# Reciprocal roots of layer norms moved to ScalarE as ln and exp, c loaded as rows, and a new order of the whole kernel

## The chip, the cores and the metric

The kernel runs on one core of a Trainium2 chip. The core has a matrix engine (TensorE, PE in the profile; its weight loads are PEld), a vector engine (VectorE, DVE), a scalar engine for table functions (ScalarE, ACT), a general engine (GpSimd, POOL), and a queue engine that issues transfers (SyncE, SP). Each engine works through its own list of instructions in order and waits on semaphores for the others. The metric is the device time of one execution in microseconds.

## The reference

x is 2048 rows of 448 values, c one row of 448. All weights and activations are bf16.

```
mod = silu(c) @ w_mod                       # six rows of 448: sa ca ga sb cb gb
h = layernorm(x) * (1 + ca) + sa
q, k, v = split(h @ wqkv)                   # 16 heads of 28
logits[i, w] = q[i] . k[i - 2 w] / sqrt(28) # w = 0..7, masked where i < 2 w
x = x + ga * ((softmax(logits) @ v) @ wo)
h = layernorm(x) * (1 + cb) + sb
y = layernorm(h)
x = x + gb * (gelu(y @ w1 + b1) @ w2 + b2)  # 1792 hidden values
layernorm(t) = (t - mean(t)) / sqrt(var(t) + 1e-5)
```

So there are three layer norms for each row: one ahead of the attention, two in a row ahead of the MLP.

## The kernel before

The 2048 rows are held as eight blocks of 128 partitions by two rows (s = 0 and 1, even and odd rows). The window of the attention steps by two rows, so even and odd rows never meet in it, and each is a sequence of 1024. Channels are split into seven pieces of 64 (`KB`), and two pieces lie on the 128 partitions at a time.

The plan is a list of operations, made by `build_plan`: each has a kind, the engines that may run it, what it reads and writes, and its PSUM buffers. There are four PSUM buffers of two banks. The sequence isn't worked out at run time: the text `ORDER` gives every operation's number and engine (P TensorE, D VectorE, A ScalarE, G GpSimd, S SyncE, X a transfer that has no instruction of its own), and `SLOTS` gives each buffer's place. An engine's own list is what `ORDER` says of it, and waits follow from reads, writes and buffers.

The stages, in the order in which they begin:

- **Start.** c is loaded into columns of 128 (`c_col`, two transfers on ACT's queue, L221 and L222, four bytes or less at a time). SyncE issues the loads of x, of w_mod and of the attention's weights. TensorE runs filler products (`fill`, L302). `f_silu` (L312) makes silu(c), `f_mcol` (L325) makes sa and ca as columns by 60 small products, and `f_mcev` brings them out of PSUM.
- **First norms.** Row blocks go in four groups of two (a0, a2, a4, a6). `ln_stats` (L349) takes mean and variance, on VectorE or, for some halves, on ScalarE (L357 to L359), adds eps (`tv`, L366), takes the power -0.5 on GpSimd (`rs`, L368) and makes -mean x rs (`nm`, L370). `normalize` (L373) writes z into `zb`. Blocks 0 to 3 are transposed on TensorE (L422), blocks 4 to 7 by a transposing transfer (L435). `modulate` (L391) applies 1 + ca and sa on the way to `hT`.
- **Weight copy.** The weights of Q and K are copied from `wst` into `wqk` with each 28 columns padded to 32 (`wpad`, L239 to L253), ten copies of 896 columns that go to VectorE, ScalarE or GpSimd.
- **Projections and attention.** `qk` (L451) makes Q and K in three chunks of columns (0 to 255, 256 to 511, 512 to 1023); in the first chunk Q's two PSUM buffers are filled piece by piece as `hT` arrives. `qkev` evicts them. `vproj` makes V in nine blocks of 114 columns (`v`, evicted by `vev`), `attention` makes logits (`lt`), their exp on ScalarE, the mask, the product with V (`po`), the division (`rec`, `onm`) and a transposition (`otr`, evicted by `oev`); `wo` is the output projection and adds to x.
- **MLP.** It runs in four chunks of two row blocks. `ln2` (L625) does both norms of a block with the functions above and transposes the result by transfer (L646, `yT`). `w1` (L666) fills a buffer, GELU on ScalarE evicts it (L673), 14 times for each chunk; `w2` (L690) follows, and `fin` (L699) adds.

ScalarE's functions come from table sets, and a load (ACT_TABLE_LOAD in the profile) stands where the next function isn't in the set that is loaded; exp and gelu are in different ones, while copies and scalings need none.

Of the kernel before, what the change touches and what calls it, by code (L numbers as in the profile page):

```python
# [8 lines left out]
FP32 = mybir.dt.float32  # L9
BF16 = mybir.dt.bfloat16  # L10
ACTF = mybir.ActivationFunctionType
# [3 lines left out]
KB = 7  # L15
# [8 lines left out]
KM = 4  # L24
# [4 lines left out]
 'fill1': 17,  # L29
 'fill2': 0,  # L30
 'fill3': 2,
# [9 lines left out]
60D 1A 49G 5S 0D 61D 68P 7S 3A 2X 6X 67G 9S 62A 8X 65G 11S 4X 10X 13S 66G 15S 17S 75D 19S 63G 76A 74D 12X 21S 64G 77D 23S 14X 69A 78D 25S 70D 79G 16X  # L41
27S 72P 71G 18X 80D 81D 82A 20X 85G 50D 52A 29S 53D 84G 51D 31S 83P 22X 73A 59G 57D 33S 86P 58A 55G 141P 24X 87D 88A 35S 56G 26X 90D 54G 142P 89A 143P
106D 28X 144P 92D 151P 30X 107A 120D 32X 34X 91D 145P 153P 105D 93G 104A 94G 152D 146P 147P 95D 119D 154A 148P 99G 208P 150D 96G 36X 149A 108D 100A
210P 97D 109G 209D 98P 110D 211A 122D 116G 226P 111A 37S 115D 112G 240P 121D 101P 227A 117S 38X 123G 241A 102D 197P 124G 113S 118X 103A 242D 237P 229P
114X 125D 228D 238A 39S 212P 130D 126A 40X 239D 198A 214P 131D 213A 199S 132S 243P 127A 215A 161P 128S 133X 230A 155P 41S 129X 162D 43S 42X 231D 45S
44X 157P 156A 47S 46X 140G 200S 48X 138D 139A 137D 201S 136G 135D 232P 134A 179S 159P 233D 158A 244D 234D 180X 165P 160A 245D 202G 203D 253P 166A 250P
163P 254A 251A 255D 181S 235P 246P 164A 252D 171P 182X 247D 236A 256P 172A 248P 257D 258D 206P 249D 183S 259P 173P 260A 184X 207D 342D 405G 341D 261P
174A 343G 169P 344G 262D 345D 360D 346G 175P 170A 185S 347D 412G 359D 186X 263P 348D 176A 266P 167P 349D 264A 361G 351D 362G 267A 177P 350D 168A 187S
363D 268D 365G 188X 364A 352D 265D 216P 353G 178A 366D 354D 269P 367D 217A 355G 279P 356D 276P 369D 280A 357S 218P 368D 277A 189S 358X 281D 220P 370G
219A 371G 278D 190X 270D 222P 372D 221A 271D 374G 373A 282P 223A 375S 272P 283D 224P 284D 273A 191S 376X 274P 225A 192X 285P 275D 385P 286A 381P 420D  # L50
287P 419D 193S 386A 204D 421G 194X 382A 383P 422G 391P 384A 288D 403P 392A 379P 423D 438D 404A 195S 401P 437D 380A 377P 196X 424D 402A 439G 425D 440G
395P 426D 378A 397P 441D 427D 396A 443G 442D 387P 398A 428D 389P 388A 429D 399P 390A 205D 430G 393P 431G 400A 305P 394A 292P 432D 444D 289P 433G 406P
# [104 lines left out]
def build_plan(cfg):  # L157
# [57 lines left out]
    def load_m(a, b, nm, bulk=False):  # L215

        load("SP", 3 * 256 * (b - a) * D, lambda g, e: e.dma_start(out=g.wmod[:, 0:3, a * D:b * D], in_=g.w_mod[0:384, a * D:b * D].rearrange("(kt p) n -> p kt n", p=128)), [(nm, 0, 3)], issue=0.65, bulk=bulk)
        load("SP", 256 * (b - a) * D, lambda g, e: e.dma_start(out=g.wmod[:, 3, a * D:b * D], in_=g.w_mod[320:448, a * D:b * D]), [(nm, 3, 4)], issue=0.42, at=lambda g: g.wmod[0:1, 3, a * D:a * D + 1])

    op("ms", {"DVE": 0.12}, lambda g: g.nc.vector.memset(g.c_col[0:64, 3:4], 0.0), wr=[("c_col", 2, 3)], bump=5000.0)  # L220
    load("ACT", 900, lambda g, e: e.dma_start(out=g.c_col[:, 0:3], in_=g.c[:, 0:384].rearrange("o (kt p) -> p (o kt)", p=128)), [("c_col", 0, 1)], issue=0.45)  # L221
    load("ACT", 900, lambda g, e: e.dma_start(out=g.c_col[64:128, 3:4], in_=g.c[:, 384:448].rearrange("o p -> p o")), [("c_col", 1, 2)], issue=0.45)  # L222
# [5 lines left out]
    load("SP", 229376, lambda g, e: e.dma_start(out=g.wst[:, 3], in_=g.A_wqkv[320:448, 0:2 * D]), [("wqk", 3, 4)], issue=0.45)  # L228
# [10 lines left out]
    for kb in range(KB):  # L239
        lo, up = ((3, k - 5) if k >= 5 else (k // 2, k % 2) for k in (kb, (kb + 1) % KB))  # L240
        if kb == 4:
            up = (2, 1)
        for halves in ([(0, 128, lo[0], 0)] if lo[0] == up[0] and (lo[1], up[1]) == (0, 1) else [(0, 64, *lo), (64, 64, *up)]):
            def f(g, kb=kb, x=halves, e=None):
                p0, n, i, h = x
                dst = g.wqk[p0:p0 + n, kb].rearrange("p m (r e) -> p (m r) e", e=32)[:, :, 0:DH]
                src = g.wst[64 * h:64 * h + n, i, :].rearrange("p (r d) -> p r d", d=DH)
                if e == "ACT":
                    g.nc.scalar.copy(out=dst, in_=src)
                else:  # L250
                    (g.nc.vector if e == "DVE" else g.nc.gpsimd).tensor_copy(out=dst, in_=src)  # L251
            i = halves[2]
# [652 lines left out]
```

## Time and profile before

| what | value |
|---|---|
| median of three runs | 180.21 us (177.99 to 181.09) |
| the profiled execution | 177.12 us, of which the span from first to last instruction is 175.4 us |
| busy share of the span | TensorE 93%, VectorE 64%, ScalarE 61%, GpSimd 39% |
| granted TensorE clock, mean | 0.99 |
| table loads on ScalarE | 6 of 1.28 us |
| first projection of Q and K | at 12.81 us |
| first `w1` product | at 72.13 us |
| first `w1` product of the second chunk | at 97.95 us |
| last `w2` product ends | at 172.05 us |

Busy shares are averages over stages with different limits. The groups of a page give busy time and the mean duration of one instruction; behind the second bar is the idle time of the engine just ahead of these instructions, with what ended it. An engine that idles costs nothing unless the last chain of work runs through it.

### The profile page before, as it was taken

How to read it: one execution, taken by the hardware profiler on the slowest of the kernel's cores; microseconds unless marked ns; L12 is line 12 of the kernel's file. 1: busy time of each engine (PE TensorE's matmuls, PEld its weight loads, DVE VectorE, ACT ScalarE, POOL GpSimd, SP SyncE). 2: the span in 40 equal slices, each digit the busy share in tenths (PEclk: the TensorE clock that was granted, in tenths of full speed). 3: DMA queues.
4: the chain of work that ended last, by engine and by line, in shares of the span. 5: the costliest groups of instructions: out<-in, count | busy, mean ns of one | idle time of the engine just before them, and what ended most of it. 6: DMA issues, size and time to landing. Idle time of an engine off the chain costs nothing.

```text
span 175.4 us, 7205 instructions
## 1 busy us (share of the span) xinstructions
PE 163.5 (93%) x3235; PEld 111.4 (64%) x3236; DVE 112.6 (64%) x234; ACT 106.9 (61%) x155; POOL 68.8 (39%) x99
## 2 busy tenths in 40 slices
PE   7889987999779988999999999999999999999992
PEld 2367754875335476699655877755589754886550
DVE  0699995594868988549798656996699812001203
ACT  2489987688334797788923686983268610686000
POOL 7594760030265454023676404623423754000400
PEclk9969999999999999999999999999999999999999
DMA  4999759628345408532024200003400044000202
GB/s 68 365 381 351 281 120 124 133 54 257 103 181 209 108 15 174 109 109 78 4 41 87 90 6 4 4 6 56 105 4 0 4 104 105 6 0 4 78 0 78
DMA packets 20939, 17.56 MB, mean 100 GB/s; under 512 B 12328, under 2 KB 19372, under 8 KB 20908
## 3 DMA queue, kind: packets, MB, share of 16 engines
q1 hardware_dynamic: 20428, 17.10, 35.3%
q8 instruction: 25, 0.41, 1.0%
q10 hardware_dynamic: 480, 0.00, 0.1%
q14 instruction: 6, 0.05, 0.1%
HBM read 12.51 MB, written 1.84 MB: 82 GB/s over the span
## 4 chain that ended last, share of the span: by engine, by line
PE 59%; DVE 15%; DMA 11%; ACT 4%; issue 4%; POOL 4%; SPq 0%; ACTq 0%; POOLq 0%; DVEq 0%
PE ps L666 25%; PE ps L690 19%; PE ps L465 7%; DMA yT<-zb 6%; DVE st L361 5%; PE ps L617 4%; DMA x_all<-in_A_x_dram 3%; DMA hT<-zb 3%; POOL rs L368 2%; PE ps L541 2%; PE ps L570 1%; DVE mv L362 1%; ACT et L549 1%; DVE zb L382 1%; DVE w L251 1%
## 5 line engine op out<-in xcount | busy, mean ns | idle before, releaser
L673 ACT ACTIVATE hmw<-ps,b1c 128x512 bf16<-128x512 f32 x56 | 38.1, 687 | 15.8 <-PE ps L666 12.6
L666 PE MATMUL ps<-yT,w 64*128 64x256 bf16 x784 | 44.4, 269 | 0.3 <-DMA yT<-zb 0.3
L690 PE MATMUL ps<-w,hmw 128*128 128x448 bf16 x224 | 43.6, 353 | 0.0
L666 PEld LDWEIGHTS <-w 64*128 64x128 bf16 x784 | 40.1, 94 | 4.1 <-issue 1.2
L690 PEld LDWEIGHTS <-hmw 128*128 128x128 bf16 x224 | 21.3, 98 | 19.8 <-issue 0.4
L465 PE MATMUL ps<-hT,w 64*128 64x256 bf16 (+1 forms) x336 | 26.4, 307 | 0.4 <-DVE hT L395 0.4
L681 POOL TENSOR_TENSOR x1p<-x_all,gbb 128x896 f32<-128x896 bf16 x8 | 15.1, 1892 | 27.7 <-DVE x_all L699 22.1
L699 DVE TENSOR_TENSOR x_all<-ps,x1p 128x896 bf16<-128x896 f32 x7 | 7.6, 1092 | 27.1 <-PE ps L690 27.1
L465 PEld LDWEIGHTS <-w 64*128 64x128 bf16 x336 | 16.2, 94 | 8.1 <-DVE hT L395 0.8
L368 POOL TENSOR_TENSOR rs<-tv,neg_half 128x2 f32<-128x2 f32 (+1 forms) x20 | 17.8, 892 | 8.1 <-DVE tv L366 4.5
L366 POOL TENSOR_SCALAR tv<-mv 128x2 f32<-128x2 f32 (+1 forms) x14 | 6.2, 445 | 31.9 <-DVE mv L362 31.9
L361 DVE BATCH_NORM_STATS2 st<-x_all 128x6 f32<-128x448 bf16 x28 | 17.1, 609 | 0.1
L549 ACT ACTIVATE et<-ps 128x912 bf16<-128x912 f32 x18 | 16.0, 934 | 1.7 <-PE ps L541 1.6
L620 DVE TENSOR_TENSOR x_all<-ps,x_all 128x896 bf16<-128x896 f32 x8 | 8.7, 1089 | 8.7 <-PE ps L617 8.7
L506 PE MATMUL ps<-wv,hT 64*64 64x448 bf16 x252 | 12.9, 350 | 0.6 <-ACT hT L393 0.6
L617 PE MATMUL ps<-wo,hT 64*128 64x448 bf16 x112 | 12.0, 350 | 0.9 <-ACT hT L601 0.9
L557 DVE TENSOR_TENSOR et<-et,mask 128x912 bf16<-128x912 bf16 x18 | 12.3, 700 | 0.2 <-ACT et L549 0.2
L601 ACT COPY hT<-ps 128x798 bf16<-128x798 bf16 x7 | 5.8, 824 | 10.8 <-PE ps L593 5.6
L506 PEld LDWEIGHTS <-hT 64*64 64x64 bf16 x252 | 8.0, 107 | 4.3 <-issue 1.2
L361 DVE BATCH_NORM_STATS2 st<-h 128x6 f32<-128x448 bf16 x16 | 9.8, 614 | 0.1
L380 POOL TENSOR_SCALAR zb<-h,rs,nm 128x448 bf16<-128x448 bf16 x10 | 8.0, 805 | 4.7 <-DMA yT<-zb 3.3
L583 DVE TENSOR_TENSOR on<-ps,rden 128x896 bf16<-128x896 f32 x9 | 9.7, 1081 | 0.3
(98 smaller groups left out, 186.2 us busy)
## 6 DMA issues: line engine op xcount, KB each, us to landing
w<-in_B_w_dram SPq DMA_DIRECT2D x3, 896.0 KB, 4.7
out_dram<-x_all SPq DMA_DIRECT2D x7, 224.0 KB, 1.9
x_all<-in_A_x_dram SPq DMA_DIRECT2D x3, 448.0 KB
hmw<-in_w_mod_dram SPq DMA_DIRECT2D x1, 1344.0 KB
w<-in_B_w_dram SPq DMA_DIRECT2D x2, 448.0 KB, 4.9
hmw<-in_w_mod_dram SPq DMA_DIRECT2D x1, 672.0 KB
wv<-in_A_wqkv_dram SPq DMA_DIRECT2D x2, 336.0 KB
wo<-in_A_wo_dram SPq DMA_DIRECT2D x2, 336.0 KB
```

The source lines that it names most:

```text
L361: g.nc.vector.bn_stats(out=g.stats[nm][:, i, :], in_=x)
L368: op(kind, {"POOL": 0.75}, lambda g: g.nc.gpsimd.tensor_tensor(out=g.rs[nm][:], in0=g.tv[nm][:], in1=g.neg_half[:, 0:n], op=ALU.pow), rd=[ ...
L465: g.nc.tensor.matmul(o[:, s, x:x + n], lhsT=g.wqk[r0:r0 + 64, kb, m, :], rhs=g.hT[r0:r0 + 64, k, c0(t0):c0(t0 + n)], start=(kb == 0 and (n ...
L506: g.nc.tensor.matmul(o[64 * half:64 * half + 64, s, 0:D], lhsT=g.hT[r0:r0 + 64, (kb + s) % KB, ka:ka + 64], rhs=g.wv[r0:r0 + 64, kb, :], s ...
L549: g.nc.scalar.activation(out=g.ebufs[et.slot][:, 912 * hf:912 * hf + 912].rearrange("p (r c) -> p r c", r=2), in_=g.ps[lt.slot][:, :, 0:8 ...
L557: g.nc.vector.tensor_tensor(out=v, in0=v, in1=g.mask[:].rearrange("p a b -> p (a b)"), op=ALU.mult)
L583: g.nc.vector.tensor_tensor(out=g.onb[rd_.slot][:].rearrange("p s (h d) -> p s h d", h=H), in0=o[:, :, :, 0:DH], in1=g.rden[rd_.slot][:].u ...
L617: g.nc.tensor.matmul(o[:, s, 0:D], lhsT=g.hT[r0:r0 + 64, (kb + s) % KB, c0(128 * j):c0(128 * j + 128)], rhs=g.wo[r0:r0 + 64, kb, :], start ...
L666: g.nc.tensor.matmul(o[:, s, 0:n], lhsT=g.w1[r0:r0 + 64, kb, ft * 128:(ft + 1) * 128], rhs=g.yTb[yT.slot][r0:r0 + 64, (kb + s) % KB, 0:n], ...
L673: g.nc.scalar.activation(out=g.hmv(hm.slot)[:, ft, :, 0:n], in_=g.ps[p1.slot][:, :, 0:n], func=ACTF.Gelu_apprx_tanh, bias=g.b1c[:, ft:ft + 1])
L681: op("x1p", {"POOL": 2.05}, lambda g, j=j, xp=xp: g.nc.gpsimd.tensor_tensor(out=g.x1pb[xp.slot][:], in0=g.x_all[:, j], in1=g.gbb2[:].unsqu ...
L690: g.nc.tensor.matmul(o[:, s, 0:D], lhsT=g.hmv(hm.slot)[:, ft, s, cc:cc + 128], rhs=g.w2[:, ft, :], start=(ft == 0), stop=(ft == FT - 1))
```

## The change

- c is loaded by one transfer as seven rows of 64 (`c7`). After four fillers TensorE multiplies it with columns of the identity, twice (`f_ct`), which puts it into columns in PSUM; ScalarE and VectorE read it there for silu. The last piece of the contraction is 64 long now, so that the last loads of w_mod and of Q's and K's weights bring 64 rows where they brought 128. `f_mcol` and the row products (`later_mod`) follow that split, and `f_mcol` goes by pieces of the contraction instead of by columns.
- Each copy of Q's and K's weights is cut into Q's half and K's half of 448 columns, with names of their own (`wqp0`, `wqp4`). GpSimd is allowed for K's half only. There are eleven of each; the new order puts Q's on VectorE (7) and ScalarE (4) and all of K's on GpSimd.
- `f_rs` joins what stood in two operations: on GpSimd the power as before, on ScalarE Ln (with eps as its bias in the first norms) and then Exp with scale -0.5.
- The eviction of the first two transposed blocks is split into seven operations, one for each piece of channels.
- `ORDER`, `SLOTS` and the counts of fillers (`fill0` 4, `fill1` 9, `fill3` 1) are new. Every engine's list changes. Nine of the 20 reciprocal roots are given to ScalarE: those of groups a0 and a4 of the first norms, both of row block 0 in the MLP's norms, the first of block 1, and both of blocks 2 and 3. The adding of eps moves to VectorE for many of the MLP's norms.

```diff
+    load("ACT", 900, lambda g, e: e.dma_start(out=g.c7[:], in_=g.c.rearrange("o (kb p) -> (o kb) p", p=64)), ["c7"], issue=0.45)
...
+        for u in range(2):
+            g.nc.tensor.matmul(g.ps[ctb.slot][64 * u:64 * u + 64, 0, 0:KM], lhsT=g.c7[:], rhs=g.ident[0:KB, u:2 * KM:2], start=True, stop=True, tile_position=(0, 64 * u))
+    cto = op("ct", {"PE": 0.3}, f_ct, rd=["c7", "ident"], uses=[ctb], mode="32x64", n=2, after=f1)
+    fill(1, cfg["fill1"], [P.buf("ps", "fill")], [cto])
...
-            op("wpad", {"ACT": 0.93, "DVE": 0.40, "POOL": 0.95}, f, rd=[("wqk", i, i + 1), "wz"], wr=[("wqp", 2 * kb + halves[0] // 64, 2 * kb + (halves[0] + halves[1]) // 64)])
+                op("wpad", {"DVE": 0.33, "ACT": 0.55, "POOL": 0.55} if m else {"DVE": 0.33, "ACT": 0.55}, f, rd=[("wqk", i, i + 1), "wz"], wr=[(f"wqp{m}", 2 * kb + halves[0] // 64, 2 * kb + (halves[0] + halves[1]) // 64)])
...
-        op(kind, {"DVE": 0.16, "POOL": 0.3}, lambda g, e="DVE": (g.nc.vector if e == "DVE" else g.nc.gpsimd).tensor_scalar_add(out=g.tv[nm][:], in0=g.mv[nm][:, :, 1], scalar1=EPS),
-           rd=[("mv" + nm, 0, n)], wr=["tv" + nm])
-        op(kind, {"POOL": 0.75}, lambda g: g.nc.gpsimd.tensor_tensor(out=g.rs[nm][:], in0=g.tv[nm][:], in1=g.neg_half[:, 0:n], op=ALU.pow),
-           rd=["tv" + nm, "nh"], wr=["rs" + nm])
+        if not act:
+            op(kind, {"DVE": 0.16, "POOL": 0.3}, lambda g, e="DVE": (g.nc.vector if e == "DVE" else g.nc.gpsimd).tensor_scalar_add(out=g.tv[nm][:], in0=g.mv[nm][:, :, 1], scalar1=EPS),
+               rd=[("mv" + nm, 0, n)], wr=["tv" + nm])
+
+        def f_rs(g, e="POOL"):
+
+            v = g.mv[nm][:, :, 1] if act else g.tv[nm][:]
+            if e == "ACT":
+                g.nc.scalar.activation(out=g.rs[nm][:], in_=v, func=ACTF.Ln, **(dict(bias=g.eps[:, 0:1]) if act else {}))
+                g.nc.scalar.activation(out=g.rs[nm][:], in_=g.rs[nm][:], func=ACTF.Exp, scale=-0.5)
+                return
+            if act:
+                g.nc.gpsimd.tensor_scalar_add(out=g.tv[nm][:], in0=v, scalar1=EPS)
+            g.nc.gpsimd.tensor_tensor(out=g.rs[nm][:], in0=g.tv[nm][:], in1=g.neg_half[:, 0:n], op=ALU.pow)
+        op(kind, {"POOL": 1.2 if act else 0.8, "ACT": 0.45}, f_rs, rd=["nh", ("mv" + nm, 0, n) if act else "tv" + nm], wr=["rs" + nm], func=EXPF)
...
-                for half, kbs in enumerate((range(0, 4), range(4, KB))):
+                for kbs in [range(kb, kb + 1) for kb in range(KB)] if js[0] == 0 else (range(0, 4), range(4, KB)):
+                    half = kbs[0] // 4
```

More of the change, by code (lines that the diff above doesn't have):

```diff
@@ L28 @@
 CFG = {'exp_phases': [5, 7, 9, 9],
- 'fill1': 17,
+ 'fill0': 4,
+ 'fill1': 9,
  'fill2': 0,
- 'fill3': 2,
+ 'fill3': 1,
  'lead': 4,
@@ L382, in f @@
                 g.nc.vector.tensor_scalar(out=dst(g), in0=src(g), scalar1=g.mv[nm][:, idx, 0:1], scalar2=g.rs[nm][:, idx:idx + 1], op0=ALU.subtract, op1=ALU.mult)
-        return op(kind, {"DVE": ndur, "ACT": 0.77, "POOL": 0.78}, f, rd=list(rd) + [k1, k2, k3], wr=wr, uses=uses)
+        return op(kind, {"DVE": ndur, "ACT": 0.77, "POOL": 0.85}, f, rd=list(rd) + [k1, k2, k3], wr=wr, uses=uses)
     names = P.names = []
```

134 lines of the change are left out of this document (66 added, 68 removed), and 6 rows, old and new, of the table SLOTS.

## The prediction

> **What bounds the kernel now.** I read the page first (span, busy shares, the chain), then the windows of each engine over stages that I cut where the trace shows a change of work, then the timeline of the first 20 us and around the table loads.
>
> ```profile
> span 175.4 us, 7205 instructions
> ...
> PE 163.5 (93%) x3235; PEld 111.4 (64%) x3236; DVE 112.6 (64%) x234; ACT 106.9 (61%) x155; POOL 68.8 (39%) x99
> ...
> PE 59%; DVE 15%; DMA 11%; ACT 4%; issue 4%; POOL 4%; SPq 0%; ACTq 0%; POOLq 0%; DVEq 0%
> ```
>
> TensorE is busy 93%, and 59% of the chain is its own; ScalarE (ACT) is busy 61% and holds 4% of the chain. So TensorE sets the time, and each engine counts only where TensorE waits for it. The windows (columns: engine busy, instructions, granted clock, DMA share, GB/s) say where that can be:
>
> ```profile
> 23.00:31.55 8.55, 6.53 (x275) 4.78 (x275) 5.92 (x16) 7.54 (x12) 2.48 (x4) 1.00 0.83 139
> ...
> 50.00:72.13 22.13, 19.88 (x543) 11.72 (x539) 16.96 (x37) 15.51 (x19) 11.91 (x13) 1.00 0.45 112
> ...
> 85.05:97.95 12.90, 12.90 (x276) 7.22 (x265) 10.80 (x17) 5.55 (x7) 8.48 (x8) 1.00 0.27 56
> 97.95:126.30 28.35, 28.17 (x638) 19.25 (x628) 20.21 (x43) 18.99 (x25) 10.62 (x14) 1.00 0.13 28
> 126.30:172.05 45.75, 45.73 (x525) 32.33 (x525) 17.36 (x38) 20.56 (x30) 12.76 (x12) 1.00 0.12 34
> ```
>
> From 72 us on it never idles (12.90 of 12.90, 45.73 of 45.75). In 23 to 72 us ACT is the fullest helper: 7.54 of 8.55, then 15.51 of 22.13.
>
> **The change, part by part.** The largest part isn't in its title. `f_rs` can now make 1/sqrt(var) on ACT as Ln, then Exp, in place of POOL's power. The new order gives ACT nine of the 20: groups a0 and a4 of the first norms; in the MLP's norms both of row block 0, the first of 1, both of 2 and of 3. In the instruction lists of the two built programs ACT loads a function table 6 times before and 23 times after: each Ln loads one set, each Exp loads the exp set back; one load for exp that stood after the first GELU chunk is replaced. The trace has the 20 too, and of the 6 loads the five behind the start (groups by line, then the timeline):
>
> ```profile
> L368 POOL TENSOR_TENSOR rs<-tv,neg_half 128x2 f32<-128x2 f32 (+1 forms) x20 | 17.8, 892 | 8.1 <-DVE tv L366 4.5
> ...
> L673 ACT ACT_TABLE_LOAD x3 | 3.8, 1283 | 3.7 <-DVE x_all L699 3.6
> ...
> L549 ACT ACT_TABLE_LOAD x2 | 2.6, 1283 | 0.1
> ...
> 85.07 1.28 ACT L549 ACT_TABLE_LOAD   x1
> 86.36 2.58 ACT L549 ACTIVATE et<-ps 128x912 bf16<-128x912 f32 x3
> 7.47 0.19 ACT L309 ACTIVATE e_c<-c_col 128x4 f32<-128x4 bf16 x1
> ```
>
> One load is 1.283 us, and the next activation starts 0.01 us after it (85.07 + 1.28, 86.36). Ln and Exp on 2 or 4 columns are not in the trace; the nearest row is the 4-column exp, 0.19. So a pair is 2 x 1.283 + 2 x 0.19 = 2.95 us of an in-order engine, and 17 more loads are 21.8 us. The Trainium skill (ScalarE: Activation LUTs, "What ACT_TABLE_LOAD costs") agrees on 1283 ns, but adds about 1380 ns of drain to every switch; by that the 17 would take 45 us and the sum below could be some 23 us longer. The 0.01 us above doesn't show the drain, so the row decides.
>
> What this does goes by four stages.
>
> *(a) Up to the first projection.* The first row is from the chain in order of time, the others from the timeline (start, duration, in brackets the wait before it):
>
> ```profile
> 1.26 4.59 DMA x_all<-in_A_x_dram
> ...
> 4.98 0.06 DVE L220 MEMSET c_col<- 64x1 bf16 x1 [3.83 <-DMA c_col<-in_c_dram]
> ...
> 6.46 0.59 DVE L361 BATCH_NORM_STATS2 st<-x_all 128x6 f32<-128x448 bf16 x1
> ...
> 7.09 0.18 DVE L362 BATCH_NORM_AGGREGATE mv<-st 128x2 f32<-128x6 f32 x1
> ...
> 7.85 1.04 POOL L368 TENSOR_TENSOR rs<-tv,neg_half 128x4 f32<-128x4 f32 x1 [1.95 <-DVE e_c L314]
> ...
> 8.32 1.44 PE L330 MATMUL ps<-silu,hmw 128*128 128x1 bf16 x52 [0.56 <-DVE silu L319]
> ...
> 8.93 0.23 DVE L370 SCALAR_TENSOR_TENSOR nm<-mv,rs 128x4 f32<-128x4 f32 x1 [0.66 <-POOL rs L368]
> ...
> 9.20 0.76 ACT L378 ACTIVATE zb<-x_all,nm,rs 128x448 bf16<-128x448 bf16 x1 [1.54 <-DVE nm L370]
> ...
> 9.53 2.79 DVE L251 COPY w<-w 128x896 bf16<-128x896 bf16 x4
> ...
> 9.99 0.94 ACT L249 COPY w<-w 64x896 bf16<-64x896 bf16 x1
> ...
> 11.10 3.99 POOL L251 COPY w<-w 64x896 bf16<-64x896 bf16 x4
> ...
> 12.24 1.35 DVE L395 TENSOR_SCALAR hT<-ps,ca_c,sa_c 128x256 bf16<-128x256 bf16 x4
> 12.68 1.48 ACT L393 ACTIVATE hT<-ps,sa_c,ca_c 128x256 bf16<-128x256 bf16 x3
> ...
> 12.81 6.99 PE L465 MATMUL ps<-hT,w 64*128 64x256 bf16 x112 [0.36 <-DVE hT L395]
> ```
>
> Before, VectorE (DVE) stands 3.83 us until c has landed. With seven rows that wait goes, but x block 1 lands at 5.85 (1.26 + 4.59) and DVE has both its halves to do: about 0.75 each, 7.4, much as now (7.09 + 0.18). The c path gains nothing. How soon the rows of c land isn't shown: between nothing and the 4.98 of now; at 4.98 its exp would hold ACT's statistics to about 7.5, so 0 to 0.1. The two tail loads of 112 KB less are 0.3 us each at 378 GB/s (the first clock row below) and nothing waits for those bytes: 0 (to -0.3).
> In the new list the first Ln's load waits for DVE's statistics. So 7.4 + 2.95 = 10.35, and 10.6 with the mean's product (0.23), where POOL had it at 8.93 + 0.23: +1.4. ACT then has two normalizations (12.1), four weight copies of half the columns (0.94 less half of 0.94 - 0.19: 0.56 each, 14.3) and a modulation (1.48 / 3): 14.8. DVE after two normalizations has seven half-width copies at 2.79 / 4 / 2 = 0.35, the eviction of sa and ca, and a modulation: 14.9. The first projection starts at 14.8 instead of 12.81, **+2.0**. K's eleven half copies on POOL (3.99 / 4 / 2 = 0.5 each from about 9) end at 15, ahead of their use at 18: 0, or up to +1 if sharing slows them. TensorE's new `ct` pair waits for c and the identity; behind it stand fillers and `f_mcol`, which waits for silu later than that: 0. The 60 products of `f_mcol` are as many as before, reordered; they end near 9.7 and are covered: 0. Fewer fillers (13 for 17, 1 for 2) lie in idle time: 0 in themselves.
>
> *(b) The second pair, a4's, stands ahead of `qkev` of Q's first half, and the first `lt` (logits) needs it.*
>
> ```profile
> 19.73 2.84 PE L506 MATMUL ps<-wv,hT 64*64 64x448 bf16 x56
> ...
> 23.00 1.03 PE L541 MATMUL ps<-qT,kT 28*64 28x57 bf16 x64
> ...
> L549 ACT ACTIVATE et<-ps 128x912 bf16<-128x912 f32 x18 | 16.0, 934 | 1.7 <-PE ps L541 1.6
> ...
> L515 ACT CAST vb<-ps 128x896 bf16<-128x896 f32 x8 | 7.2, 903 | 1.9 <-PE ps L506 1.9
> L481 ACT CAST qT<-ps 128x1024 bf16<-128x1024 f32 x7 | 7.1, 1015 | 4.1 <-PE ps L465 4.1
> ```
>
> The projection ends at 14.8 + 7.0 = 21.8, the first V block (2.84 / 2) at 23.2, its eviction 24.1, the pair 27.1, the eviction 28.1: `lt` then, where it was at 23.0. Two `lt`, a normalization (0.76), two exps (0.93) and two more `lt` end at 31.4; before, the same products would have been through at about 28.0 (31.55 less two V blocks and one `po`). The lag is 3.4, so **+1.4** here. POOL, freed of nine powers, has no one waiting for it: 0. SP issues the four transposes of the first norms in another order (blocks 6, 7, 4, 5):
>
> ```profile
> 35.73 1.68 POOL L395 TENSOR_SCALAR hT<-hT,ca_c,sa_c 128x512 bf16<-128x512 bf16 x2 [9.76 <-DMA hT<-zb]
> ```
>
> Their modulation, five of seven on POOL now instead of two, takes 5 x 0.84 = 4.2 from then on, where three engines shared it; the chunk of projection behind it starts 3 us or more later too (the lag of (b)), so 0, from above 2.
>
> *(c) Four pairs lie between the logits of block 3 and the first GELU.* ACT's 15.51 in the window 50 to 72.13 becomes 15.51 + 4 x 2.95 = 27.3; two normalizations (1.5) and an eviction (0.9) move off it: 24.9. That is more than 22.13: **+2.8**. From above, if what moved off comes back as other evictions and DVE's order makes the loads wait: 5.2. From below 0, if ACT's 6.6 us of idle takes it.
>
> *(d) Three pairs lie between the last GELU of chunk 0 and the y of chunk 1.* The first and the last row are from the chain:
>
> ```profile
> 68.32 3.67 DMA yT<-zb
> ...
> 85.26 8.16 PE L690 MATMUL ps<-w,hmw 128*128 128x448 bf16 x42
> ...
> 97.95 3.23 PE L666 MATMUL ps<-yT,w 64*128 64x256 bf16 x56
> ...
> 101.18 1.32 PE ps L617 x14
> ```
>
> The queue on ACT is: pair, four exps, pair, normalization, pair, normalization, 3 x 2.95 + 4 x 0.93 + 2 x 0.76 = 14.1, 14.5 with the two waits for DVE's mean product; then the transposing DMA, 3.67: the first `w1` 18.2 us after the GELUs. Before it is 12.9 (85.05 to 97.95), all filled by TensorE; the new order puts one `wo` (1.32) and one `otr` (28 small products, 0.4 by the 64 `lt` in 1.03) more ahead: 14.6. **+3.6**; from below 0, if the second norms of blocks 2 and 3 end early, from above 5.3.
>
> After 98 us ACT has no more pairs and TensorE's work is the same 74 us: 0.
>
> Sum: 2.0 + 1.4 + 2.8 + 3.6 = 9.8 us. The profiled execution took 177.12 (175.4 of span and 1.7 around it) and would take 186.9; it lies 3.1 below the median of the runs shown, 180.21, to which I add the same: **190.0**.
>
> **Rivals.**
> *Absorbed.* ACT idles 68.5 of 175.4 us, and a load that stands in a wait costs nothing. If (c) and (d) vanish, 3.4 remain: 183.6. Against it: in (c) the sum exceeds the window, and in (d) the pairs stand in the path of y.
> *One set serves both (not slower).* If Ln and Exp ran without loads, a pair were 0.4 us against 1.04 of POOL's power plus its add: the first norms come at 7.4 + 0.4 + 0.2 = 8.0 where they came at 9.2, the projection starts at about 12.2 and nothing waits later: -0.6 to -1.2, 179.3. It decides at the count of loads: 6 or fewer. Against it: the built list names two set numbers in turn, and that list had the right 6 before. The Trainium skill (ScalarE: Activation LUTs, "Table sets: the hidden batching unit") states this case: a set with both functions makes ln then exp one load; the trace has no Ln, so it can't say.
> *Dearer.* If ACT bounds (c) from above, 5.2, and TensorE's new idle times lower its clock, it grows. The clock does fall here after the sparse 7.8 to 10 us:
>
> ```profile
> 11.00:12.00 1.00, 0.90 (x8) 0.88 (x9) 0.97 (x2) 0.95 (x5) 0.94 (x2) 0.50 1.05 378
> ...
> 13.65:14.00 0.35, 0.35 (x8) 0.35 (x9) 0.35 (x1) 0.35 (x2) 0.35 (x1) 1.00 1.09 364
> ```
>
> That is half speed for up to 3.3 us (10.4 to 13.65), so 1.6 us lost; three such after the gaps of (a), (c) and (d) are 4.8. With 2.4 more in (c) and 1.7 in (d): 199.
>
> **How the numbers follow.** Forecast 0.66 (187 to 194 by itself), absorbed 0.14, one set 0.07, dearer 0.13. Range 183.5 to 199, from the absorbed case to the dearer one, with one set below it and little above. A measurement of this kernel tells about 2% from no change: 176.6 to 183.8. Under it lies a small part of one set (0.02); within it the rest of one set and half of absorbed (0.12); slower 0.86.
>
> **What would show it.** In the profile after: 23 table loads, two of them ahead of each ACT row of `rs`; ACT busy about 130 us; the first projection (L482) near 14.8; a gap on TensorE before the first `lt`; gaps of some us between 50 and 80 and ahead of the second chunk's `w1`; none behind that. POOL's power 11 times. Fewer loads, or TensorE without gaps in spite of them, would prove me wrong; so would an equal count with the loads all inside waits.

## The result, and the profile after

The changed kernel takes 200.12 us (median of 4 runs, 199.32 to 201.58), the kernel before 179.1 us beside it (4 runs): a ratio of 1.121, 95% interval 1.108 to 1.134. So it is 21 us slower, where 9.8 was forecast. (Ratios, here and below, leave out runs more than about 1.5% above the fastest of their kernel, so a median of all runs and a ratio can differ a little.) Its profiled execution took 201.58 us, 24.5 more than that of before (177.12). From the page of the changed kernel (span, busy time of each engine, granted clock in 40 slices, chain by engine, and the groups of the table loads of the pairs):

```profile
span 199.9 us, 7212 instructions
...
PE 170.4 (85%) x3233; PEld 112.6 (56%) x3233; DVE 116.8 (58%) x252; ACT 127.6 (64%) x178; POOL 54.9 (27%) x90
...
PEclk9957975998599995589999999999999999999998
...
PE 57%; ACT 18%; DVE 7%; DMA 6%; issue 5%; SPq 4%; POOL 1%; ACTq 0%
...
L378 ACT ACT_TABLE_LOAD x9 | 11.5, 1283 | 0.8 <-DVE mv L366 0.7
L379 ACT ACT_TABLE_LOAD x9 | 11.5, 1283 | 0.2
```

There are 18 loads in the nine pairs (with five others 23, as forecast), and ACT is busy 127.6 us (forecast about 130). ACT's share of the chain went from 4% to 18%. The clock row has holes: half speed in slices 3, 7, 11 and 16 to 17 (of 5 us each), where before only slice 3 was low, at 0.6.

The span is TensorE's busy time and its idle time. Its products are the same but for a few fillers and the two products that turn c. Busy went from 163.5 to 170.4 (+6.9, with a mean clock of 0.92 instead of 0.99), idle from 11.9 to 29.5 (+17.6). The windows by stage say where. I cut at three marks that both kernels have: the first product by `wo`, the first `w1`, the first `w1` of the second chunk. Columns as before: length, then TensorE, its weight loads, VectorE, ACT, GpSimd busy, clock, DMA share, GB/s. Before:

```profile
0.00:46.84 46.84, 40.91 (x940) 27.23 (x942) 33.46 (x75) 34.73 (x61) 21.48 (x48) 0.96 0.73 206
...
46.84:72.13 25.29, 22.90 (x602) 13.21 (x594) 19.87 (x41) 15.51 (x19) 12.23 (x13) 1.00 0.49 131
72.13:97.95 25.82, 25.81 (x550) 19.41 (x550) 21.12 (x39) 17.07 (x22) 11.68 (x13) 1.00 0.30 73
97.95:172.03 74.08, 73.89 (x1163) 51.59 (x1152) 37.57 (x80) 39.55 (x54) 23.38 (x25) 1.00 0.12 32
```

After:

```profile
0.00:53.08 53.08, 39.17 (x849) 26.89 (x849) 33.86 (x82) 34.78 (x55) 23.85 (x57) 0.83 0.68 174
...
53.08:91.81 38.73, 30.75 (x659) 15.55 (x656) 23.22 (x50) 25.91 (x31) 6.82 (x7) 0.84 0.30 85
91.81:124.39 32.58, 28.48 (x624) 20.25 (x622) 21.95 (x41) 28.02 (x40) 3.83 (x6) 1.00 0.22 57
124.39:196.43 72.04, 72.02 (x1112) 49.92 (x1109) 37.18 (x79) 38.93 (x54) 20.42 (x21) 1.00 0.14 33
```

The stages differ by +6.2, +13.4, +6.8 and -2.0 us. (The marks don't cut quite the same work. Of the eight groups of 14 products of the projection's last chunk, three stand ahead of the first `wo` before and one after; a group takes 1.7 us at full clock, so by estimate some 3.4 us of work moved from the first stage into the second, and like for like these two differ by about 9.6 and 10. And TensorE's busy time in the last stage is 1.9 less, for work that the new order does earlier.) TensorE's idle time is 13.9 instead of 5.9 in the first, 8.0 instead of 2.4 in the second, 4.1 instead of nothing in the third. In the second stage neither engine is full: TensorE idles 8.0 us and ACT 12.8 of 38.73.

The places, from the timeline of TensorE after (start, duration, in brackets the wait before it):

```profile
14.29 7.95 PE L482 MATMUL ps<-hT,w 64*128 64x256 bf16 x112 [1.79 <-DVE hT L410]
...
28.72 0.93 PE L558 MATMUL ps<-qT,kT 28*64 28x57 bf16 x64 [2.82 <-ACT qT L498]
...
50.12 3.17 PE L482 MATMUL ps<-hT,w 64*128 64x512 bf16 x14 [3.79 <-DVE hT L620]
...
63.19 0.41 PE L610 MATMUL ps<-ident,on 57*64 57x57 bf16 x28 [1.90 <-ACT qT L498]
...
72.19 1.52 PE L523 MATMUL ps<-wv,hT 64*64 64x448 bf16 x28 [0.41 <-ACT qT L498]
...
77.52 0.58 PE L610 MATMUL ps<-ident,on 57*64 57x57 bf16 x28 [3.82 <-ACT kT L498]
...
121.06 0.63 PE L610 MATMUL ps<-ident,on 57*64 57x57 bf16 x56 [2.66 <-DVE on L600]
...
124.39 0.93 PE L683 MATMUL ps<-yT,w 64*128 64x256 bf16 x14
```

And the rows of the other engines that stand behind four of these waits:

```profile
5.81 1.28 ACT L378 ACT_TABLE_LOAD   x1 [0.69 <-DVE mv L366]
7.11 0.30 ACT L378 ACTIVATE rs<-mv,eps 128x4 f32<-128x4 f32 x1
...
9.98 2.52 POOL L249 COPY w<-w 64x448 bf16<-64x448 bf16 x4 [3.21 <-DMA w<-in_A_wqkv_dram]
...
47.16 2.40 DVE L738 TENSOR_TENSOR wo<-wo,ga 128x3136 bf16<-128x3136 bf16 x1 [1.82 <-DMA ga<-mdr]
...
72.15 1.28 ACT L378 ACT_TABLE_LOAD   x1
74.85 0.20 ACT L378 ACTIVATE rs<-tv 128x2 f32<-128x2 f32 x1 [1.42 <-DVE tv L371]
75.07 1.28 ACT L379 ACT_TABLE_LOAD   x1
...
119.45 0.16 DVE L385 SCALAR_TENSOR_TENSOR nm<-mv,rs 128x2 f32<-128x2 f32 x1 [2.46 <-ACT rs L379]
```

One wait was not in the forecast at all: the 3.79 us ahead of 50.12. TensorE waits for `oev.1`, the eviction on VectorE that writes into `hT`; it stands behind the scaling of wo by ga, and that waits for ga.

### The profile page after: what moved, and what is told of

Same layout as the page of the kernel before. It is cut to its first block, busy times and chain, and to the rows that moved or that the text cites. A ratio compares the mean times of both kernels' runs of the same rounds, so it can differ in the third digit from the quotient of the medians.

```text
span 199.9 us, 7212 instructions
## 1 busy us (share of the span) xinstructions
PE 170.4 (85%) x3233; PEld 112.6 (56%) x3233; DVE 116.8 (58%) x252; ACT 127.6 (64%) x178; POOL 54.9 (27%) x90
## 4 chain that ended last, share of the span: by engine, by line
PE 57%; ACT 18%; DVE 7%; DMA 6%; issue 5%; SPq 4%; POOL 1%; ACTq 0%
PE ps L683 21%; PE ps L707 17%; PE ps L482 9%; PE ps L634 5%; ACT L378 5%; ACT L379 3%; PE ps L523 3%; ACT et L566 3%; DMA wo<-in_A_wo_dram 2%; DMA ga<-mdr 2%; SPq L452 2%; ACT qT L498 1%; DVE st L365 1%; DMA x_all<-in_A_x_dram 1%; DVE w L249 1%
## 5 line engine op out<-in xcount | busy, mean ns | idle before, releaser
L690 ACT ACTIVATE hmw<-ps,b1c 128x512 bf16<-128x512 f32 x56 | 37.3, 688 | 11.9 <-PE ps L683 9.1
L683 PEld LDWEIGHTS <-w 64*128 64x128 bf16 x784 | 39.1, 94 | 5.3 <-issue 1.5
L482 PE MATMUL ps<-hT,w 64*128 64x256 bf16 (+1 forms) x336 | 31.9, 350 | 5.6 <-DVE hT L620 3.8
L482 PEld LDWEIGHTS <-w 64*128 64x128 bf16 x336 | 18.5, 106 | 15.5 <-issue 4.8
L365 DVE BATCH_NORM_STATS2 st<-x_all 128x6 f32<-128x448 bf16 x29 | 17.7, 609 | 2.5 <-DMA x_all<-in_A_x_dram 2.4
L634 PE MATMUL ps<-wo,hT 64*128 64x448 bf16 x112 | 14.3, 401 | 1.9 <-ACT hT L618 1.8
L371 POOL TENSOR_SCALAR tv<-mv 128x2 f32<-128x2 f32 x7 | 1.6, 232 | 48.6 <-DVE mv L366 48.6
L498 ACT CAST kT<-ps 128x1024 bf16<-128x1024 f32 x8 | 8.1, 1011 | 9.5 <-PE ps L482 9.5
L385 DVE SCALAR_TENSOR_TENSOR nm<-mv,rs 128x2 f32<-128x2 f32 (+1 forms) x20 | 3.1, 154 | 17.6 <-ACT rs L379 17.5
L574 DVE TENSOR_TENSOR et<-et,mask 128x912 bf16<-128x912 bf16 x18 | 11.4, 649 | 3.1 <-ACT et L566 3.0
L383 POOL TENSOR_TENSOR rs<-tv,neg_half 128x2 f32<-128x2 f32 (+1 forms) x11 | 10.0, 910 | 11.1 <-DVE tv L371 10.6
L634 PEld LDWEIGHTS <-hT 64*128 64x128 bf16 x112 | 5.8, 106 | 9.5 <-ACT hT L618 3.6
```

Of the source, the lines that this page charges most:

```text
L365: g.nc.vector.bn_stats(out=g.stats[nm][:, i, :], in_=x)
L482: g.nc.tensor.matmul(o[:, s, x:x + n], lhsT=g.wqk[r0:r0 + 64, kb, m, :], rhs=g.hT[r0:r0 + 64, k, c0(t0):c0(t0 + n)], start=(kb == 0 and (n ...
L574: g.nc.vector.tensor_tensor(out=v, in0=v, in1=g.mask[:].rearrange("p a b -> p (a b)"), op=ALU.mult)
L634: g.nc.tensor.matmul(o[:, s, 0:D], lhsT=g.hT[r0:r0 + 64, (kb + s) % KB, c0(128 * j):c0(128 * j + 128)], rhs=g.wo[r0:r0 + 64, kb, :], start ...
L683: g.nc.tensor.matmul(o[:, s, 0:n], lhsT=g.w1[r0:r0 + 64, kb, ft * 128:(ft + 1) * 128], rhs=g.yTb[yT.slot][r0:r0 + 64, (kb + s) % KB, 0:n], ...
L690: g.nc.scalar.activation(out=g.hmv(hm.slot)[:, ft, :, 0:n], in_=g.ps[p1.slot][:, :, 0:n], func=ACTF.Gelu_apprx_tanh, bias=g.b1c[:, ft:ft + 1])
```

## The experiments

All kernels compute the whole reference. Ratios are to the kernel before, run on the same chip beside them; only these are compared across groups. The words of `ORDER` are an operation's number and its engine's letter.

**One table set for ln and exp.** A set that holds both functions is loaded by hand where the next activation of that kind follows another set, so the loads fall from 23 to 6 and nothing else changes. The second kernel takes the nine roots as powers on GpSimd again, in the new order.

```diff
 for o in order:
     if o.fn is None:
         continue
+    if o.eng == "ACT" and o.func and o.func != table:
+        if o.func == EXPF:
+            nc.scalar.preload_act_table_set("natural_log_exp_and_others")
+        table = o.func
```

```diff
-... 89A ... 122A ... 356A ... 365A ... 374A ... 434A ... 452A ... 443A ... 461A ...
+... 89G ... 122G ... 356G ... 365G ... 374G ... 434G ... 452G ... 443G ... 461G ...
```

> The changed kernel, with the set that holds both ln and exp loaded by hand wherever an exp-like function follows another set: 6 table loads instead of 23, nothing else moved. Theory 1 (the 17 loads, the stalls behind them and the lower TensorE clock that follows are the whole loss): 178 to 182 us, a ratio of 0.99 to 1.015 to the kernel before, mean granted clock 0.97 or more, ACT busy about 106 us. Theory 2 (the new order of the queues, ga's late arrival above all, makes a loss of its own): 186 to 192 us, and the stall of TensorE behind the scaling of wo stays.

> The changed kernel with the nine reciprocal roots given back to GpSimd's power, at the same places of the order. Theory 1 (the table loads): 179 to 184 us, a little behind the one-set kernel, since a power with its add is 1.3 us against 0.4. Theory 2 (the order): 186 to 192 us. If moving the roots off GpSimd mattered by itself, this would be more than 3 us slower than the one-set kernel.

One set: 185.27 us, ratio 1.038 (1.028 to 1.047), between the two theories. Powers: 184.96 us, 1.030 (1.020 to 1.040). So by the ratios (1.121 and 1.038) the loads are worth 14.9 of the 21 us, the rest of the change costs 6.7 us without them, and where the roots are taken is worth nothing that can be told once the loads are gone. The windows of the one-set kernel, by the same marks:

```profile
0.00:50.27 50.27, 38.95 (x847) 26.87 (x849) 32.80 (x82) 29.55 (x51) 23.84 (x57) 0.86 0.73 185
...
50.27:80.71 30.44, 27.77 (x659) 14.45 (x656) 23.16 (x50) 17.74 (x26) 6.83 (x7) 0.95 0.37 111
80.71:108.88 28.17, 28.16 (x626) 20.12 (x623) 21.70 (x41) 19.38 (x31) 3.83 (x6) 1.00 0.29 62
108.88:180.91 72.03, 72.01 (x1112) 49.60 (x1109) 37.18 (x79) 38.93 (x54) 20.40 (x21) 1.00 0.14 33
```

This kernel has the changed kernel's order, so the two differ by the loads alone: by stage 2.8, 8.3, 4.4 and 0, together 15.5 us for loads of 21.8 us. ACT's busy time differs by 5.2, 8.2, 8.6 and 0. So in the second stage each microsecond of load is one of the stage, though ACT idles a third of it; in the first and the third about half of the loads' time is paid. The timeline says where the second stage pays. The three products that waited for an eviction on ACT in the changed kernel (1.90, 0.41 and 3.82 us) are these in the one-set kernel:

```profile
58.85 0.41 PE L610 MATMUL ps<-ident,on 57*64 57x57 bf16 x28
...
67.36 1.52 PE L523 MATMUL ps<-wv,hT 64*64 64x448 bf16 x28
...
69.70 0.41 PE L610 MATMUL ps<-ident,on 57*64 57x57 bf16 x28 [0.83 <-ACT kT L498]
```

Their waits fell from 6.1 to 0.8 us. That is all of the 5.3 us by which TensorE idles less here; the other 3.0 are its busy time, at a clock of 0.95 instead of 0.84.

**The same roots in the order of before.** Five of the roots of before (79, 109, 344, 353, 362; the first norms of a0 and a4, in the MLP both of row block 0 and the first of block 1) go from GpSimd to ScalarE as ln and exp, nothing else; then the same with one set (the diff above).

```diff
+def f_rs(g, e="POOL"):
+    if e == "ACT":
+        g.nc.scalar.activation(out=g.rs[nm][:], in_=g.tv[nm][:], func=ACTF.Ln)
+        g.nc.scalar.activation(out=g.rs[nm][:], in_=g.rs[nm][:], func=ACTF.Exp, scale=-0.5)
+        return
...
-... 79G ... 109G ... 344G ... 362G ... 353G ...
+... 79A ... 109A ... 344A ... 362A ... 353A ...
```

> The kernel before, in its own order, with five of its reciprocal roots (a0, a4, both of row block 0, the first of block 1) as Ln and Exp on ScalarE in the places where GpSimd had the power: 16 table loads for 6. If a load costs what it takes of ACT's time where ACT is the fullest helper, and nothing where it idles: +4 to +9 us on the kernel before (182 to 188 us). If the loads hurt only together with the new order: within 2 us of the kernel before.

> The same five roots on ScalarE in the order of before, with the set loaded that holds ln and exp: 6 loads. A pair is then 0.4 to 0.5 us against 0.7 to 1.0 on GpSimd: 0 to -1 us on the kernel before. If ACT minds even the short pairs: +1 to +2 us.

With loads 189.06 us, ratio 1.062 (1.049 to 1.075); with one set 180.73, 1.020 (1.012 to 1.029). By the ratios ten loads (12.8 us) cost 7.4 us here, by the medians 8.3: about 60% of their time. Both kernels are slower than was expected of them either way: roots on ScalarE without any loads don't gain but cost 2%, and no run shows why. The second stage, with loads and then with one set:

```profile
53.36:84.14 30.78, 25.00 (x601) 14.27 (x594) 19.35 (x41) 24.20 (x31) 9.04 (x10) 0.89 0.40 107
```

```profile
49.28:74.56 25.28, 22.87 (x604) 13.63 (x594) 20.01 (x41) 16.66 (x26) 9.85 (x10) 1.00 0.47 131
```

Three pairs are in it: ACT +7.5, the stage +5.5 us. So here the stage hides about a quarter of the loads.

**The clock.** 57 filler products, on a zero tile of their own, in five of TensorE's gaps of the changed kernel.

```diff
+names = {153: (0, 6), 238: (1, 10), 187: (3, 16), 271: (1, 8), 284: (2, 17)}
...
+if o.i in names:
+    slot, n = names[o.i]
+    for k in range(n):
+        nc.tensor.matmul(g.ps[slot][:, k % 2, 0:512], lhsT=g.zz[:], rhs=g.zz[:, 0:1].to_broadcast([128, 512]), start=True, stop=True)
```

> The changed kernel with 57 filler products of 512 columns on TensorE in its five long gaps (6 ahead of the first projection, 10 ahead of the first logits, 16 ahead of the third chunk's first projection, 8 and 17 ahead of two transpositions), in PSUM buffers that are free then. No wait goes. If the lower clock behind the gaps is a loss of its own (TensorE's busy time rose by about 8 us with fewer fillers): 193 to 197 us, clock 0.97 or more. If the clock doesn't matter, because the work behind a gap waits for ACT anyway: 199 to 201 us.

199.03 us, 1.116 (1.108 to 1.125), which isn't told apart from the changed kernel's 1.121. The clock rose from 0.92 to 0.964. The second stage fell from 38.7 to 34.3 us, but the first grew by 1.1 and the third by 1.7. In the first, fillers stand ahead of work that is ready: the projection's third chunk starts at 52.68, 2.1 us after the eviction that it needs (49.98 + 0.57). The third has no fillers in it; behind the same pause of 2.66 us the clock, which stayed at 1.00 in the changed kernel, was halved this time (0.50 from 120 to 122). So the half clock is real in the second stage, and this is no way to get it back.

**ga and the eviction, one by one.** The load of ga (212S) right behind the last transposing DMA (130S), in the changed kernel and in the one-set kernel; then also `oev.1` (259D) issued behind the projection (187P) that waited for it. That last edit changes no engine's own order. The two touch different columns of `hT`; the wait between them turns round, so that the eviction now waits for the projection (1.20 us in the trace) and TensorE doesn't wait for the eviction.

```diff
-... 130S 38S ... 212S 45X ...
+... 130S 212S 38S ... 45X ...
...
-... 263A 259D 187P 193S ...
+... 263A 187P 259D 193S ...
```

> The changed kernel with one word of the order moved: the broadcast load of ga goes on SyncE's queue right behind the transpose of block 5, ahead of two loads of wo, those of the other rows, of b1 and of b2. Loads of tables as in the changed kernel. Theory 2 (a queue order that costs of itself): the stall of 3.8 us at 46 to 50 us and the half-clock spell behind it (about 2.6 us) go, 193.5 to 196 us. Theory 1 (only the table loads count): the stall is taken over by the next wait on ACT, 198 to 200 us.

> The one-set kernel (185.3 us) with ga's load moved on SyncE's queue as in the third run. There the scaling of wo waits for ga alone by the trace (44.97 us, TensorE idle from 44.2 to 47.3, half clock to 52). If ga is what is late, 180 to 182 us; if wo itself lands no earlier than that, as in the run with the loads, 184.5 to 186 us.

> The run before this one with one more word moved: the eviction of the attention's block 1 (oev.1, on VectorE behind the scaling of wo) is written after the third chunk's first projection, so that this projection doesn't wait for it. If the written place of that eviction, and not ga, makes the stall: 179.5 to 181.5 us and no gap at 44 to 47 us; if TensorE only moves the gap to wo, which needs the eviction anyway: 183 to 185 us.

ga early: 203.32 us, 1.140 (1.132 to 1.148); with one set 185.94, 1.051 (1.043 to 1.058); and with the eviction 184.96, 1.045 (1.038 to 1.053). None gains, and the first is above both of its expectations. The scaling of wo in the first of them:

```profile
48.68 1.79 DVE L738 TENSOR_TENSOR wo<-wo,ga 128x3136 bf16<-128x3136 bf16 x1 [1.34 <-DMA gate<-wo]
```

It now waits for wo itself. In the third kernel TensorE's wait for the eviction, 2.47 us without that edit, is gone, and what stays is 2.19 us for b1r (2.01 without it), another load at the end of the same queue. The theory "ga is late" fell; what is late is everything that SyncE issues behind its transposes.

**SyncE's queue and the start.** On the one-set kernel: the copies of wo and b1r ahead of the transposes of blocks 4 and 5, ga behind these (wo first); 13 instead of 9 and 5 instead of 1 filler products at the start; both; both with the powers on GpSimd.

```diff
-... 34S ... 144S ... 36S ... 126S ... 130S 38S ... 40S ... 42S ... 212S ...
+... 34S 35X 36S ... 144S 37X 38S 40S 42S ... 126S ... 130S 212S ...
...
- 'fill1': 9,
+ 'fill1': 13,
...
- 'fill3': 1,
+ 'fill3': 5,
```

> One table set, and the copies of wo go ahead of the transposing DMAs on SyncE's queue, with b1r and ga behind them. Theory (SyncE's in-order queue makes the gap of TensorE at 44 to 47 us of the one-set kernel, because wo, ga and b1r land late): the last copy of wo is issued near 33 us instead of 37.5, ga near 38 instead of 41.2, the gap of 3.05 us ahead of the first projection by wo shrinks below 1 us, the half clock behind it goes, and the time falls from 185.3 to 180 to 182 us. Rival (the queue isn't the cause, the gap follows from the late start, or the transposes of block 2, now later, make another): the gap moves or stays and the time is 184 to 186 us.

> One table set, and 4 filler products more behind the columns of c and 4 more ahead of the first projection. Theory (the first projection is long because TensorE's clock is halved from 10 to 18 us): its 112 products take about 7.0 us, as in the kernel before, instead of 8.74, and the time falls by 1 to 2 us to 183.5 to 184.5. Rival (the projection goes at the pace of the weight copies): it takes 8 us or more whatever the clock, and the time stays at 185 to 186 us.

> The two edits together. Theory: both gains add, 178.5 to 181 us, about the kernel before. Rival (one wait takes the place of the other): 183 to 186 us.

> The two edits on the kernel that takes the nine roots on GpSimd as powers again, so without any pair on ScalarE. Theory (where the roots are taken is worth nothing once the table loads are gone): within 1% of the kernel with both edits and one set. Rival (ScalarE's load matters): faster than it by 2 us or more.

185.91 (1.047, 1.025 to 1.069), 184.84 (1.041, 1.021 to 1.061), 184.15 (1.041, 1.030 to 1.052) and 184.83 us (1.044, 1.030 to 1.058): no gain that can be told. Yet in the kernel with both edits what they aimed at moved. The window of 15 to 20 us in the one-set kernel, then in the kernel with both edits (the clock is the third number from the end):

```profile
15.00:20.00 5.00, 5.00 (x57) 4.11 (x55) 4.65 (x14) 4.00 (x13) 3.24 (x6) 0.58 1.05 332
```

```profile
15.00:20.00 5.00, 5.00 (x96) 4.96 (x94) 4.65 (x15) 4.43 (x13) 3.26 (x6) 1.00 1.00 329
```

And the timeline of the one-set kernel, then that of the kernel with both edits, with the wait that comes next in it:

```profile
14.14 8.74 PE L482 MATMUL ps<-hT,w 64*128 64x256 bf16 x112 [2.23 <-DVE hT L410]
```

```profile
14.11 6.45 PE L482 MATMUL ps<-hT,w 64*128 64x256 bf16 x112 [2.25 <-DVE hT L410]
...
39.08 1.11 DVE L410 TENSOR_SCALAR hT<-hT,ca_c,sa_c 128x512 bf16<-128x512 bf16 x2 [3.84 <-DMA hT<-zb]
...
41.25 0.16 PE L745 MATMUL ps<-ident,b1r 14*128 14x14 bf16 x1 [2.30 <-DVE vb L534]
```

The first projection goes at full clock and 2.3 us shorter, and the last copies of wo are issued from 30.30 us instead of 36.09. But now the transposes of blocks 4 and 5 are late (3.84 us on VectorE) and TensorE stops there. Nor do the fillers keep the clock up each time: in the trace of the kernel with the fillers alone it is at 0.50 from 12 to 18 us and the projection takes 7.95.

**All of it.** The transposes of blocks 4 and 5 ahead of the last copies of wo; the shift and scale columns copied earlier on VectorE (84D from behind six weight copies to behind two); and the wait for `oev.1` taken away as above. An expectation below calls this last edit "moved ahead" of the scaling; in fact the eviction stays behind the scaling, and the projection no longer waits for it.

```diff
-... 144S 37X 38S 40S 42S ... 126S ... 211S ... 130S 212S ...
+... 144S ... 129D 126S 130S 211S 37X 38S 40S 42S 212S ...
...
-... 51D 96P ... 63D 84D ... 98A 97D ...
+... 51D 84D 96P ... 63D 97D ... 98A ...
```

> As the run with both edits (184.15 us), with the transposing DMAs of blocks 4 and 5 ahead of the last copies of wo on SyncE's queue. Theory (one in-order queue serves both, so with wo first the transposes came late: VectorE stood 3.84 us for them until 39.1 us and TensorE 2.30 us behind it): VectorE's modulation starts before 37 us, the pause of TensorE at 39 to 41 us goes, and the time is 181 to 183 us. Rival (then wo or its gates land late again and the pause comes back at the first projection by wo): 184 to 185 us.

> As the run with both edits, with the copies of the shift and scale columns moved on VectorE from behind six weight copies to behind two, and the first modulation ahead of the last weight copy. Theory (the new order of VectorE at the start, not the norms, delays the first projection: the columns were copied at 12.46 us and ScalarE waited 0.79 us for them): the first projection starts near 13.0 us instead of 14.1 and the time falls by about 1 us to 183. Rival (the weights' landing or the later copies of Q's half set the start): it starts at 13.8 us or later, or takes as much longer, and the time stays at 184 us.

> All of these edits, and the evacuation that stood behind the scaling of wo on VectorE moved ahead of it. Theory (what is left of the change beside its table loads is the order of the start and of SyncE's queue): 178.5 to 181.5 us, within 1% of the kernel before. Rival (the pauses of TensorE between 35 and 50 us are in the order of its own work and stay, whatever queue is cleared): 183 to 184.5 us.

> The same edits, but the table loads left as in the changed kernel (23). Theory (the loads cost their own time at the points where TensorE waits behind ScalarE, whatever the queues do): 14 to 16 us above the run with all edits, 194 to 197 us. Rival (much of the 15 us of the loads was that they pushed the transposes, and with them wo, back on SyncE's queue): 6 to 11 us above it.

> As the run with the start filled and wo first (184.15 us), and the evacuation oev.1 issued behind the projection that waited for it; no engine's own order changes by that, only this wait goes. If this wait is what held the 3 us between that run and the run with all edits (181.21 us): 181 to 182.5 us. If the queue's order or the columns were needed too: 183.5 to 184.5 us.

> The run with all edits without the early copies of the shift and scale columns: filled start, transposes ahead of the last copies of wo, and the wait for oev.1 gone. Theory (columns early gained nothing alone, so it isn't them): 181 to 182.5 us. If they were needed: 183.5 us or more.

| on both edits above | us | ratio (95%) |
|---|---|---|
| transposes first | 185.44 | 1.034 (1.025 to 1.043) |
| columns early | 184.52 | 1.035 (1.023 to 1.047) |
| no wait for `oev.1` | 182.52 | 1.018 (1.010 to 1.026) |
| transposes first, no wait | 180.19 | 1.011 (1.006 to 1.016) |
| all three | 181.21 | 1.010 (1.000 to 1.020) |
| all three, with the 23 loads | 194.0 to 200.8 in four runs | |

Columns early does nothing: the first projection then waits for a weight copy on GpSimd (0.72 us) and starts at 14.13. Taking away the wait for `oev.1`, which gained nothing beside the early ga, gives 2.3% once wo and b1r are early, and 2.3% again with the transposes first (1.034 to 1.011). Putting the transposes first on top is not told apart from it (the intervals overlap). The stages of the kernel with all three:

```profile
0.00:44.17 44.17, 36.62 (x854) 25.45 (x855) 32.18 (x81) 30.15 (x52) 23.36 (x57) 1.00 0.75 206
```

```profile
44.17:74.90 30.73, 28.00 (x658) 14.66 (x658) 24.55 (x52) 16.73 (x25) 7.19 (x8) 0.94 0.40 112
74.90:103.06 28.16, 28.15 (x624) 20.12 (x622) 21.70 (x41) 19.37 (x31) 3.82 (x6) 1.00 0.29 67
103.06:175.10 72.04, 72.02 (x1112) 49.73 (x1109) 37.18 (x79) 38.94 (x54) 20.43 (x21) 1.00 0.14 33
```

Against the one-set kernel the first stage is 6.1 us shorter and the others are equal within 0.3: all that these edits win back lies ahead of the first product by `wo`. The second stage still has a clock of 0.94, behind a wait of 2.99 us at its start. With the loads back in this order the runs spread too far for a ratio, but each is 12.8 us or more above 181.21, so the loads' price isn't one of pushing SyncE's queue back (6 to 11 us). No kernel tried beats the kernel before.

## Why the prediction was wrong

The direction was right, and the 17 more loads are the larger part of the loss; the size was half. Two steps failed: the price of (c), where the loads cost 8.3 us and not 2.8, and the nothing put on SyncE's queue: of the 6.7 us that the change costs without its loads, a new order of that queue, with the wait for `oev.1` and the fillers at the start, wins back about 4.8 (1.038 to 1.011). The forecast had 3.4 us up to the lag of (b), 2.8 for (c), 3.6 for (d); the stages show 6.2, 13.4 and, the last two together, 4.7 (of the 13.4, some 3.4 is work that stood in the first stage before).

- **(a) +2.0, near in size, wrong in its reason.** The first projection starts at 14.29 (forecast 14.8; before 12.81). But the statistics start at 3.43 and don't wait for x after that, so the pair was done at 8.92 and the weights, landing at 9.98, came last: GpSimd had waited 3.21 us for them. Without the loads it starts at 14.14, so this delay is nearly all the new order's and not the pair's, and the near hit is luck. Behind that step the projection took 1.0 us longer than before (7.95 for 6.99), which was costed at nothing: the clock is at 0.50 up to 17.7 us, before up to 13.5, and at full clock the same products take 6.45. A half copy takes 0.44 us on VectorE (2.65 / 6), not 0.35, and 0.63 on GpSimd (2.52 / 4), not 0.5.
- **(b) right.** The first `lt` is at 28.72 (forecast 28.1), behind a pair and the eviction of Q.
- **SyncE's queue, "0, from above 2": wrong.** Transposes wait for z, z waits behind ACT's second pair, and wo, b1r and ga stand behind the transposes. The first transpose is issued at 29.39 instead of 23.83, and still at 27.80 without the loads, so most of this is the order. The prediction followed the transposes to their own reader (the modulation) and not what is queued behind them. TensorE's idle time ahead of `wo` grew from 5.9 to 11.3 us without the loads and to 13.9 with them.
- **(c) +2.8 is the step that failed in the price of the loads.** It set ACT's sum (24.9) against the window (22.13) and counted only the excess, as if ACT could fill its idle time. In this stage it didn't: evictions wait for products and products for evictions, in turn, so a block on ACT's queue delays the next eviction and the products behind it (the waits of 1.90, 0.41 and 3.82 us, which shrink to 0.83 without the loads). The loads in this stage cost 8.3 us: 5.3 as idle time of TensorE (8.0 against 2.7) and 3.0 as busy time at lower clock (30.75 against 27.77). Nor are there four pairs in it, but three and the start of the fourth, whose first load is at 90.98. The rest of the +13.4, 5.1 us, is there without the loads too, as 4.9 more of TensorE's busy time: some 3.4 is the work that stood in the first stage before, and the rest goes with a clock of 0.95 (the first `wo` takes 2.82 us in the one-set kernel, 1.50 before).
- **(d) +3.6, right in size, by another last wait.** GELUs end at 106.06, the first `w1` of the second chunk is at 124.39: 18.3 us, forecast 18.2; in the one-set kernel it is 14.65 (94.23 to 108.88), where 14.6 was forecast for the new order alone. ACT's queue is as it was forecast. The last wait is not the transposing DMA, though, but VectorE's division ahead of `otr` (2.66), which stands on VectorE behind a mean product that waits 2.46 us for the third pair.
- **Behind it nothing**: as forecast, TensorE doesn't idle (72.02 of 72.04).
- **The rivals.** "One set" was right as a mechanism that this kernel does not have: loaded by hand it takes 6 loads and 185.3 us, not 179.3, since the order itself costs 3.8%. "Dearer" (199) came nearest: it named the half clock and more in (c), but not the queue. The drain that the Trainium skill adds to a load (ScalarE: Activation LUTs, "What ACT_TABLE_LOAD costs") isn't seen here either: the Ln behind the load of 5.81 starts at 7.11, 0.02 us after it, and the load of 72.15 starts 0.02 us after the eviction ahead of it (71.14 + 0.99).

What stays open: which part of the remaining 1% of the best variants is the start (a first projection 0.2 to 2.3 us later than before in them) and whether the transposes' place matters by itself. c as rows and the halved weight copies were not taken back one by one, so no run gives them a price of their own.

## What to carry to other kernels

Where two in-order engines hand work to each other in turn, don't subtract the idle time of one from a block put on it: here the loads of such a stage cost 8.3 us for 8.2 in one order and 5.5 for 7.5 in the other. Even a stage in which TensorE never waits without the loads (the third, 28.16 of 28.17) paid 4.4 for 8.6. When a transfer on a queue comes to wait for something new, list everything behind it on that queue with its reader, since the first late one that is cured only shows the next. And before two functions are put on ScalarE as a pair, count the table loads in the built program: here one hand-placed set was worth 15 us.

## What the runs showed of the hardware that was not expected

A VectorE operation on 2 columns took 1.75 us, beside one of GpSimd:

```profile
72.90 1.89 POOL L698 TENSOR_TENSOR x1p<-x_all,gbb 128x896 f32<-128x896 bf16 x1
73.07 1.75 DVE L371 TENSOR_SCALAR tv<-mv 128x2 f32<-128x2 f32 x1
```

They end within 0.03 us of each other (74.79 and 74.82), and the table load's Ln waited 1.42 us for it. The same line took 0.16 to 0.30 us at its eight other places in the changed kernel. The Trainium skill (SBUF — State Buffer, "Who interferes with whom") says that GpSimd and a VectorE operation that uses both of its port pairs share one pair, that whoever issues first has it for its whole instruction, and that the other is blocked. The times in the trace agree; which ports the small operation used it doesn't show.

TensorE's clock was halved behind the pauses of 2.82, 3.79 and 3.82 us of the changed kernel, about 2 us after each began, and products then ran at half speed for 5 to 8.5 us (up to 34.8, 55.3 and 86.0): 3.17 us for 14 products at 50.12, where 1.67 to 1.69 is usual. Behind 1.90 us it was not. The length of the pause alone doesn't settle it: behind the same 2.66 us it stayed at 1.00 here and was halved in the kernel with 57 fillers.
